# First pair prepared head by head, first two heads' minima and marks re-ordered, scores eight slots behind their minima

## The chip, the cores and the metric

One NeuronCore of a Trainium2 chip runs the whole program. The metric is device time in microseconds (us) of one execution; the kernel before has a median of 839.23 us over three executions (838.45 to 841.17).

## The reference, cut to what matters

Clustered attention (2 batches, 8 heads, 768 tokens, head width 64, 16 centroids a head), then two feed-forward blocks:

```python
q_assign = argmax(q_n @ c_n.T); k_assign = argmax(k_n @ c_n.T)     # q_n, k_n, c_n: rows over their norm
mask     = q_assign[..., :, None] == k_assign[..., None, :]
scores   = where(mask, q @ k.T / 8, -1e9)
attn     = softmax(scores);  x = attn @ v                          # heads side by side: 1536 x 512
x = ((x @ w1) * (x @ w2)) @ w3 @ w_out                             # 512 -> 1024 -> 1024 -> 512
y = softplus(x @ w_in) @ w_out2                                    # 512 -> 2048 -> 512
```

## The kernel before, in words

Heads go two by two: 16 heads are 8 pairs, pair `pi` holds heads `2*pi` and `2*pi+1`. A head has six *slots* of work, one for each 128 queries, 96 slots in all. The attention's main loop is one Python loop over a step `s`, in a manual schedule: each engine's instructions stand in the order in which the loop writes them. A step does, in this order, the **minima** of slot `s` (`mx_pe`: two matmuls of queries against keys, `mx_red`: VectorE takes the minimum of 128x768, since scores are kept negated), the row of minima of a head (`m_row`, every sixth step: transpose, negate, a DMA of 3 KB into row 96 of the head's query tile), the preparation of coming pairs (tables `PE` and `EV`, and `PE1`, `EV1` for pair 1), the **scores** of slot `s - ML` (`st_pe`: four matmuls, the second of each pair with row 96 in it; `st_exp`: ScalarE), and the **values** of the slot before that one (`av_pe`). `ML` is 9. From step 9 on, `w_step` puts in a piece of the product `w3 @ w_out`, which is computed here as 24 units (`wseq`: 8 of `w_out`, 16 of `w3`), one every 5/2 steps.

Preparing a pair takes: loads of q and k (`load_qk`, tile `rawqk`); transposes (`t1_pe`, unit `u` is half a head: u = 0, 1 the first head, 2, 3 the second) that ScalarE and VectorE copy out as a rounded part `H` and a remainder `L` (`t1_ev`); DMAs that lay `H` and `L` into the query and key tiles `q` and `k` (`t_dma`, seven DMAs a head, 1.18 MB by the shapes in the code); the squares of q and k (`norm_sq`), their sums, roots and reciprocals (`norm_sum`, `norm_root`, `norm_rec`); products with the centroids (`sims_pe`, tile `cst`), copied to `sT` (`sims_ev`) and turned (`simsT_pe`); `assign`, a chain of VectorE operations that ends in one-hot marks `oh`; `back_pe`, which turns the marks; and their copy into rows 96 on of `q` and `k`, for pair 0's first head straight from PSUM (`back_ev`), for the others by way of `sg` and DMAs (`m_dma`). A head's minima cannot start before its marks have landed. Ahead of the loop stand the centroids' preparation (`centroid_prep`, `centroid_turn`), pair 0's preparation for both heads at once, and four weight units.

All loads and copies go through SyncE's (SP's) queue in program order, unless `act_dma` names ScalarE's. PSUM tiles are `sb` (scores, and every second minimum of the first nine slots), `mb` (minima), `avb` (values), and three banks `rb` that `take` and `give` hand round.

Of the kernel before, what the change touches and what calls it, by code (L numbers as in the profile page):

```python
# [27 lines left out]
def fused_kernel(ctx: ExitStack, tc, q, k, v, centroids, w1, w2, w3, wo, w_in, w_o2, out):  # L28
# [132 lines left out]
    woh = xp_.tile([P, CC, DM], F32R, tag="x1", name="woh")  # L161

    def xs_of(c, bl):

        o, e = bl * BLK, bl * BLK + BLK
        for b in range(B):
            lo, hi = max(o, b * S), min(e, b * S + S)
            if lo < hi:
                yield slice(lo - o, hi - o), XT[b][:, c, lo - b * S : hi - b * S]
# [64 lines left out]
    def centroid_turn():  # L234
# [45 lines left out]
    def norm_root(pi):  # L280

        fl = PR["n", pi].rearrange("p t c n j -> p t (c n j)")
        nc.vector.tensor_scalar_max(fl[:, 1], fl[:, 0], 1e-30)
        nc.scalar.activation(fl[:, 2], fl[:, 1], AF.Ln)
        nc.scalar.activation(fl[:, 1], fl[:, 2], AF.Exp, scale=0.5)

    def norm_rec(pi, i):
        fl = PR["n", pi].rearrange("p t c n j -> p t (c n j)")
        if i == 0:
            nc.vector.reciprocal(fl[:, 2], fl[:, 1])  # L290
        elif i == 1:
            nc.gpsimd.tensor_tensor(out=fl[:, 0], in0=fl[:, 0], in1=fl[:, 2], op=ALU.mult)
            nc.gpsimd.tensor_tensor(out=fl[:, 0], in0=fl[:, 0], in1=fl[:, 1], op=ALU.add)
        else:
            nc.vector.tensor_scalar(
                out=fl[:, 2], in0=fl[:, 0], scalar1=0.5, scalar2=1e-6,
                op0=ALU.mult, op1=ALU.add,
            )
            nc.vector.reciprocal(fl[:, 3], fl[:, 2])

    def t1_pe(pi, u):
# [5 lines left out]
        m = take()  # L307
# [7 lines left out]
    def t1_ev(pi, u):  # L315
# [3 lines left out]
        hv, lv = PR["H", j][:, sl], PR["L", j][:, sl]  # L319
        nc.scalar.activation(hv, m[:, :HALF], AF.Copy, scale=qkcol[:, 0:1])  # L320
        nc.vector.scalar_tensor_tensor(
            out=lv, in0=m[:, :HALF], scalar=qkcol[:, 0:1], in1=f32(hv),
            op0=ALU.mult, op1=ALU.subtract,
        )
        give(m)

    def t_dma(pi, j):
# [5 lines left out]
        if hd:  # L333
# [3 lines left out]
        if hd:  # L337
            dma(f32(qt[:D]), a[:D].unsqueeze(1).to_broadcast([D, 2, S]))
            dma(f32(kt[:D, 0, :]), a[D:])
        else:  # L340
            dma(f32(qt[:D, 1, :]), a[:D])
        dma(f32(kt[:D, 1, :]), l[D:])
        for n in range(2 if hd else 1):
            n = 1 - n
# [8 lines left out]
    def t_first():  # L353

        a, l = f32(PR["H", 0]), f32(PR["L", 0])
        t_tiles(0)
        act_copy(QT[0][:D, 0, :], a[:D])
        act_copy(KT[0][:D, 0, :], a[D:])
        nc.gpsimd.tensor_copy(KT[0][D : D + 32, 0, :], a[D : D + 32])
        nc.gpsimd.tensor_copy(QT[0][D : D + 32, 0, :], l[:32])  # L360

    SG = ((0, 512), (512, S))

    def sims_pe(pi, g):
# [6 lines left out]
        for j in range(2):  # L371
            for t in (PR["H", j], PR["L", j]):
                nc.tensor.matmul(
                    m[:, : c1 - c0], cst[:, h0 + j, :], t[:, c0:c1],
                    start=(n == 0), stop=(n == 3),
# [9 lines left out]
    NG = 4  # L385
    NA = NG * QC

    NS = NA * NCL

    def simsT_pe(pi):  # L390
        PR["sx"] = take()
        for c in range(QC):
            nc.tensor.matmul(
                PR["sx"][:, c * NG * NCL : (c + 1) * NG * NCL],
                PR["sT"][:, c * P : (c + 1) * P], halves.rearrange("p g b -> p (g b)"),
# [3 lines left out]
    def assign(pi, i):  # L399

        s = PR["sx"][:, :NS].rearrange("p (a b) -> p a b", b=NCL)
        tt = nc.vector.tensor_tensor
        if i == 0:
            mx = PR["mx"] = ap1.tile([P, 2, NA], F32, tag="mx", name=f"mx{pi}")
            rn = PR["n", pi].rearrange("p t c n j -> p t (c n j)")[:, 3]
            tt(out=s, in0=s, in1=rn.unsqueeze(2).to_broadcast([P, NA, NCL]), op=ALU.mult)
            nc.vector.tensor_reduce(out=mx[:, 0], in_=s, op=ALU.max, axis=AX.X)
            tt(
                out=s, in0=s, in1=mx[:, 0].unsqueeze(2).to_broadcast([P, NA, NCL]),
# [22 lines left out]

    def back_ev(pi):

        if pi == 0:
            for ni, d in enumerate((QT, KT)):
                r = slice(64 * ni, 64 * ni + 32)
                nc.scalar.activation(
                    d[0][96:, 0, :], PR["bk"][r, :S], AF.Copy, scale=bigcol[r, 0:1]
                )  # L440
# [138 lines left out]
    NWSTEP = 5 * (NW - 1) // 2 + 11  # L579
# [30 lines left out]
    ML = 9  # L610
# [4 lines left out]
    def mx_bank(s):  # L615

        return sbank if s < ML and s % 2 else mbank

# [88 lines left out]
    def x_norm(u):  # L707
        g, hf = divmod(u, 2)
        b, h = divmod(g, H)
        if b not in XT:  # L710
            assert wk[0] > NWSTEP - 4
            XT[b] = xp_.tile([P, CC, S], F32, tag="x1", name="xT1")
# [3 lines left out]
            out=XT[b][rs, h // 2, cs],  # L716
# [155 lines left out]
    def steps(tab, s):  # L872
        for pi in range(2, NPAIR):
            for d in (0, 2):
                for f, *a in tab.get(s - 2 * QC * pi - d, ()):
                    if (d == 2) == (pi == 2 and f in NORM) and (f is not load_qk or pi > 2):
# [7 lines left out]
    EV1 = {  # L884
        0: [(t1_ev, 0), (norm_sq, 0)], 1: [(t1_ev, 1), (norm_sum, 0)], 2: [(t1_ev, 2), (norm_sq, 1), (t_dma, 0)],
        3: [(t1_ev, 3), (norm_sum, 1), (norm_root,)], 4: [(sims_ev, 0), (norm_rec, 0), (norm_rec, 1)],
        5: [(sims_ev, 1), (norm_rec, 2), (t_dma, 1)], 7: [(assign, 0)], 8: [(assign, 1)],
        9: [(back_ev,)], 10: [(m_dma, 0), (m_dma, 1)],
# [3 lines left out]
    WALL = "AbdsThlmpqe"  # L892
    WSLOT = 76
    W0 = 4
    wk = [W0]

    with tc.manual_schedule():
# [14 lines left out]
        t1_ev(0, 2)  # L912
        t1_ev(0, 3)
        centroid_turn()
        norm_sq(0, 0)
        norm_sq(0, 1)
        load_qk(1)
        t_first()
        sims_pe(0, 0)
        sims_pe(0, 1)  # L920
        sims_ev(0, 0)
        sims_ev(0, 1)
        norm_sum(0, 0)
        norm_sum(0, 1)
        simsT_pe(0)
        norm_root(0)
        for n in range(W0):
            w_step(n, WALL[:1])
        norm_rec(0, 0)
        norm_rec(0, 1)  # L930
        norm_rec(0, 2)
        t_dma(0, 1)
        t_dma(0, 0)
        assign(0, 0)
        assign(0, 1)
# [3 lines left out]
        w_load()
        load_v(0)  # L940
        for n in range(W0):
            w_step(n, WALL[1:])
        for s in range(NSLOT + ML + AL):
            j = s - ML
            a = j - AL
            if s < NSLOT:
                mx_pe(s)
                mx_red(s)
            if s and s % QC == 0 and s <= NSLOT:
                m_row(s // QC - 1)  # L950
            weights = s >= ML
# [4 lines left out]
            for tab in (PE1, EV1):  # L956
                for f, *x in tab.get(s, ()):
                    f(1, *x)
            if s == 4:
                load_qk(2)  # L960
            if s == 8:
                load_v(1)
            steps(PE, s)
            steps(EV, s)
            if 0 <= j < NSLOT:
                st_pe(j)
                st_exp(j)
            if weights:
# [7 lines left out]
            for g in range(NH):  # L976
                r = s - (ML + AL + QC * g + QC - 1)
# [7 lines left out]

            if wk[0] > NWSTEP and s >= WSLOT:
                i, k = divmod(s - WSLOT, 3)
# [8 lines left out]
    for g in range(NH):  # L996
        r0 = NSLOT + ML + AL - (ML + AL + QC * g + QC - 1)
# [199 lines left out]
```

## Time and profile before

| | us |
|---|---|
| median of three executions | 839.23 (838.45 to 841.17) |
| profiled execution, its own time | 842.76 |
| its span in the trace | 840.9 |
| first minima start on PE | 27.85 |
| first minima of head 1, of head 2 | 38.51, 58.03 |
| attention's last matmuls give way to the feed-forward block | 368 to 370 |

PE is TensorE's matmuls, DVE VectorE, ACT ScalarE, POOL GpSimd, SP SyncE. A row of the timeline gives start and duration; "[1.97 <-ACT k L438]" behind it is the engine's idle time just before and what ended it. The chain of waits is followed back from the last instruction, so an entry there is on the path that ended last.

### The profile page before, as it was taken

Reading aid. Unit: us, or ns where it says so; the run is one execution under the profiler, and the core shown is the slowest. Engines: PE = TensorE matmul, PEld = TensorE weight load, DVE = VectorE, ACT = ScalarE, POOL = GpSimd, SP = SyncE. Lnnn points to the kernel's source line nnn. Section 1 sums busy time; section 2 is a strip of 40 time slices with the busy share of each in tenths; the row PEclk is TensorE's granted clock in tenths of the full one; section 3 lists DMA queues with packets and bytes.
Section 4 is the critical chain, followed back from the end, with each engine's and each line's share of the span. In section 5 each row is a group of like instructions: output and inputs, shape, how many; then the busy total and the mean of one; then the engine's idle time right before and its main releaser. Section 6 shows DMA issues by size and latency. Waiting matters only on the chain.

```text
span 840.9 us, 10003 instructions
## 1 busy us (share of the span) xinstructions
PE 796.8 (95%) x3553; PEld 635.5 (76%) x3553; DVE 450.6 (54%) x754; ACT 396.5 (47%) x683; POOL 240.7 (29%) x232
## 2 busy tenths in 40 slices
PE   3679999989999999999999999999998999999997
PEld 2457777867777777778888888887786888888886
DVE  5867565475756565335332343345878644454443
ACT  3345445455453445455333245345555544454443
POOL 4145241245223122145201213222444222222220
PEclk9679999999999999999999999999999999999999
DMA  6875665465552564026301224330210100001001
GB/s 162 203 154 154 161 147 161 122 148 157 152 121 67 133 156 120 21 90 204 127 1 50 83 69 130 120 101 1 75 51 1 50 1 1 1 12 39 1 0 51
DMA packets 77490, 75.60 MB, mean 90 GB/s; under 512 B 46336, under 2 KB 62848, under 8 KB 77440
## 3 DMA queue, kind: packets, MB, share of 16 engines
q1 hardware_dynamic: 75476, 73.84, 32.5%
q10 hardware_dynamic: 1964, 1.12, 0.5%
q8 instruction: 28, 0.46, 0.2%
q14 instruction: 22, 0.18, 0.1%
HBM read 50.41 MB, written 3.24 MB: 64 GB/s over the span
## 4 chain that ended last, share of the span: by engine, by line
PE 77%; DVE 13%; DMA 3%; ACT 3%; SPq 2%; issue 2%; POOL 1%; DVEq 0%; ACTq 0%; POOLq 0%
PE avb L668 11%; PE rb L834 8%; PE sb L834 8%; PE sb L653 6%; PE sb L1059 6%; PE mb L1128 6%; PE rb L1059 5%; PE rb L533 5%; PE mb L856 4%; PE mb L623 3%; PE rb L1128 3%; PE avb L1128 3%; DVE mn L632 2%; PE avb L856 2%; PE rb L856 2%
## 5 line engine op out<-in xcount | busy, mean ns | idle before, releaser
L668 PE MATMUL avb<-E,v 128*128 128x384 f32 x384 | 142.7, 494 | 0.4 <-ACT t L61 0.4
L632 DVE TENSOR_REDUCE mn<-mb 128x1 f32<-128x768 f32 x92 | 87.7, 953 | 103.4 <-PE mb L623 103.0
L76 POOL TENSOR_TENSOR u<-u,t 128x512 f32<-128x512 f32 x47 | 66.2, 1409 | 173.1 <-DVE u L1082 173.1
L660 ACT ACTIVATE E<-sb 128x768 f32<-128x768 f32 x96 | 77.6, 808 | 70.1 <-PE sb L653 69.2
L653 PE MATMUL sb<-q,k 128*128 128x384 f32 (+1 forms) x384 | 91.4, 361 | 4.5 <-ACT E L660 4.5
L668 PEld LDWEIGHTS avb<-E,v 128*128 128x128 f32 x384 | 71.9, 192 | 28.7 <-ACT t L61 2.3
L653 PEld LDWEIGHTS sb<-q,k 128*128 128x128 f32 (+1 forms) x384 | 67.3, 194 | 9.6 <-ACT E L660 7.2
L623 PE MATMUL mb<-k,q 128*128 128x384 f32 x184 | 65.9, 440 | 8.0 <-DVE mn L632 4.1
L1059 PE MATMUL sb<-ys,wh_i 128*128 128x512 f32 x192 | 64.1, 395 | 3.6 <-ACT t L1070 2.9
L1072 DVE TENSOR_SCALAR u<-t 128x512 f32<-128x512 f32 x48 | 25.5, 531 | 71.3 <-ACT t L1071 71.3
L1059 PE MATMUL rb<-ys,wh_i 128*128 128x512 f32 x192 | 63.4, 392 | 0.0
L834 PE MATMUL rb<-xs,wh 128*128 128x512 f32 x192 | 61.7, 393 | 0.0
L834 PE MATMUL sb<-xs,wh 128*128 128x512 f32 x192 | 61.7, 392 | 0.0
L76 POOL TENSOR_TENSOR wl_o<-d_o,wh_o 128x512 fp32r<-128x512 f32 x16 | 21.2, 1327 | 122.3 <-ACT wh_o L61 116.2
L623 PEld LDWEIGHTS mb<-k,q 128*128 128x128 f32 x184 | 34.1, 198 | 26.7 <-DVE mn L632 7.2
L1081 ACT ACTIVATE u<-u 128x512 f32<-128x512 f32 x48 | 30.4, 633 | 42.4 <-DVE t L1078 42.2
L715 POOL TENSOR_TENSOR xT<-t,R 64x384 f32<-64x384 f32 x32 | 33.3, 1061 | 52.6 <-DMA R<-rd 52.3
L79 DVE TENSOR_TENSOR gl<-u,gh 128x512 fp32r<-128x512 f32 x48 | 37.8, 788 | 15.7 <-ACT gh L61 15.2
L1059 PEld LDWEIGHTS sb<-ys,wh_i 128*128 128x128 f32 x192 | 35.9, 188 | 13.3 <-ACT t L1070 3.9
L1059 PEld LDWEIGHTS rb<-ys,wh_i 128*128 128x128 f32 x192 | 36.1, 188 | 8.0
L834 PEld LDWEIGHTS rb<-xs,wh 128*128 128x128 f32 x192 | 36.1, 188 | 7.8
L834 PEld LDWEIGHTS sb<-xs,wh 128*128 128x128 f32 x192 | 36.1, 188 | 7.8
(202 smaller groups left out, 1730.9 us busy)
## 6 DMA issues: line engine op xcount, KB each, us to landing
w3r<-in_moe_w_dram SPq DMA_DIRECT2D x16, 512.0 KB
w12r<-in_moe_w_dram SPq DMA_DIRECT2D x16, 512.0 KB
wir<-in_moe_w_in_dram SPq DMA_DIRECT2D x16, 512.0 KB
wor<-in_moe_w_out_dram SPq DMA_DIRECT2D x16, 512.0 KB
q<-H SPq DMA_DIRECT2D x15, 384.0 KB
w3r<-in_moe_w_out_dram SPq DMA_DIRECT2D x8, 512.0 KB
k<-L SPq DMA_DIRECT2D x16, 192.0 KB
v<-in_v_dram SPq DMA_DIRECT2D x16, 192.0 KB
```

Source lines behind the costliest of these rows:

```text
L76: nc.gpsimd.tensor_tensor(out=o, in0=i, in1=hi, op=ALU.subtract)
L79: return nc.vector.tensor_tensor(out=o, in0=i, in1=hi, op=ALU.subtract)
L533: nc.tensor.matmul(m, a[:, ks], bb, start=(mc == 0 and x == 0), stop=(mc == NK - 1 and x == 2))
L623: nc.tensor.matmul(bank[:, hf, :HALF], QT[g][:, 0, c * P : (c + 1) * P], KT[g][:, 0, hf * HALF : (hf + 1) * HALF], start=True, stop=True,)
L632: nc.vector.tensor_reduce(out=MN[g][:, c : c + 1], in_=mx_bank(s)[:, :, :HALF], op=ALU.min, axis=AX.XY)
L653: nc.tensor.matmul(sbank[:, i, :HALF], KT[g][: P - 31 * n, n, ks], QT[g][: P - 31 * n, n, qs], start=(n == 0), stop=(n == 1),)
L660: nc.scalar.activation(E[j], sbank[:, :, :HALF], AF.Exp, scale=-1.0)
L668: nc.tensor.matmul(avbank[:, :HALF], V[g][:, 2 * kp + i, :], e[:, i, :], start=(kp == 0 and i == 0), stop=(kp == 2 and i == 1),)
L834: nc.tensor.matmul(bk[:, :BLK], a[:, sl], bb, start=(n == 0), stop=(n == 3 * CC - 1))
L856: nc.tensor.matmul(ybank[e][:, :BLK], a[:, es], bb, start=(fc == 0 and n == 0), stop=(fc == NFC - 1 and n == 2),)
L1059: nc.tensor.matmul(hbank[(bl * NF2 + fc) % 4][:, :BLK], a[:, sl], bb, start=(n == 0), stop=(n == 3 * CC - 1))
L1128: nc.tensor.matmul(ob, a[:, sl], bb, start=(fc == 0 and n == 0), stop=(fc == NF2 - 1 and n == 2),)
```

## The change

Pair 0 is now prepared one head at a time: the second half of norms, products, `assign` and `back_pe` for head 1 moves into the loop (table `PE0`, `EV0`). The loop's step is now called `o`. Steps 0 to 11 do minima 0 to 11, steps 12 and 13 none, steps 14 to 16 two each, and from step 17 on the minimum is `o + 1`, while scores are `o - 7` and values `o - 8`. Pair 1's preparation moves from steps 0 to 10 to steps 6 to 13, pair 2's has tables of its own (steps 12 to 21). Weight units start at step 14 with one every 9/4 steps and none are worked on before the loop. Head 0's query and key tile is filled by DMA instead of by ACT and POOL; the rounded part of `cst` is written by ACT; the centroids are loaded on ACT's queue; the attention results of batch 1's first two heads get a tile of their own (`xT10`).

```diff
     def centroid_load():
-        dma_in(PR["cw"], centroids.rearrange("h c d -> (h c) d"))
+        nc.scalar.dma_start(PR["cw"], centroids.rearrange("h c d -> (h c) d"))
...
-                nc.vector.tensor_scalar(
-                    out=hi, in0=mv[:, :, j, :], scalar1=sc, scalar2=None, op0=ALU.mult
-                )
+                act_copy(hi, mv[:, :, j, :], scale=sc)
...
+    def back_first():
+
+        r = slice(0, 32)
+        nc.scalar.activation(QT[0][96:, 0, :], PR["bk"][r, :S], AF.Copy, scale=bigcol[r, 0:1])
+        nc.vector.tensor_copy(KT[0][96:, 0, :], PR["bk"][64:96, :S])
+        give(PR["bm"])
...
-            for x in WT[wseq[n][0]].get(k - 5 * n // 2, ""):
+            for x in WT[wseq[n][0]].get(k - 9 * n // 4, ""):
...
-    ML = 9
+    ML = 8
...
-        0: [(t1_pe, 0)], 1: [(t1_pe, 1)], 2: [(t1_pe, 2)], 3: [(t1_pe, 3)], 4: [(sims_pe, 0)],
-        5: [(sims_pe, 1)], 6: [(simsT_pe,)], 9: [(back_pe,)],
+        6: [(t1_pe, 0)], 7: [(t1_pe, 1)], 8: [(t1_pe, 2)], 9: [(t1_pe, 3)], 10: [(sims_pe, 0)],
+        11: [(sims_pe, 1)], 12: [(simsT_pe,)], 13: [(back_pe,)],
...
+        12: [(assign, 0), (assign, 1)], 13: [(back_ev,), (m_dma, 0), (m_dma, 1)],
...
+    PE2 = {
+        13: [(t1_pe, 0)], 14: [(t1_pe, 1)], 15: [(t1_pe, 2)], 16: [(t1_pe, 3)],
+        17: [(sims_pe, 0), (sims_pe, 1)], 18: [(simsT_pe,)], 21: [(back_pe,)],
+    }
...
-    WSLOT = 76
-    W0 = 4
+    WSLOT = 81
+    W1 = 14
...
-        w_load()
-        w_load()
         t1_pe(0, 0)
         t1_pe(0, 1)
         centroid_prep()
+        norm_sq(0, 0)
+        norm_sq(0, 1)
         t1_ev(0, 0)
         t1_ev(0, 1)
+        centroid_turn()
         t1_pe(0, 2)
-        t1_pe(0, 3)
...
+        t1_pe(0, 3, avbank)
+        t1_hi(0, 2)
+        t1_hi(0, 3)
+        t_dma(0, 0, [0])
         load_qk(1)
...
+        norm_sum(0, 0)
+        sims_pe(0, 0, [0])
+        sims_pe(0, 1, [0])
+        norm_root(0, 0)
+        t1_lo(0, 2)
...
+        simsT_pe(0, slice(0, 4, 2))
+        for _ in range(3):
+            w_load()
+        load_v(0)
+        assign(0, 0, 0)
+        assign(0, 1, 0)
+        back_pe(0)
+        t1_lo(0, 3)
+        t_dma(0, 1)
+        back_first()
...
+        PE0 = {
+            0: [(sims_pe, 0, [1]), (sims_pe, 1, [1])], 1: [(simsT_pe, J1)], 4: [(back_pe,)],
+        }
+        EV0 = {
+            0: [(sims_ev, 0), (sims_ev, 1), (norm_rec, 0, 1), (norm_rec, 1, 1)],
+            1: [(norm_rec, 2, 1)], 2: [(assign, 0, 1)], 3: [(assign, 1, 1)],
+            4: [(back_ev,), (m_dma, 1)],
+        }
+        firsts = [[i] for i in range(12)] + [[], [], [12, 13], [14, 15], [16, 17]]
+        for o in range(NSLOT + ML + AL - 1):
+            s = o + 1 if o >= len(firsts) else -100
+            mxs = firsts[o] if s < 0 else [s] if s < NSLOT else []
+            j = o - ML + 1
...
+            if s < 0:
+                if o in (6, 12):
+                    m_row(o // 6 - 1)
+            elif s % QC == 0 and s <= NSLOT:
...
             if 0 <= j < NSLOT:
                 st_pe(j)
                 st_exp(j)
+            for i in mxs[1:]:
+                mx_pe(i)
+                mx_red(i)
```

The program order itself, at three places. First PE, from head 0's turned marks on. In these rows `mb` and `sb` with k and q are minima, `rb<-identF,rawqk` are transposes, `rb<-H,cst` and `rb<-L,cst` products with the centroids, `rb<-halves,sT` their turn. Before:

```order
L430 MATMUL rb_102<-identB,oh 128x128
L623 MATMUL mb<-k_213,q_212 128x384 x2
L309 MATMUL rb_100<-identF,rawqk_207 128x128 x3
L623 MATMUL sb<-k_213,q_212 128x384 x2
L309 MATMUL rb_101<-identF,rawqk_207 128x128 x3
```

The same place of the changed program:

```order
L440 MATMUL rb_101<-identB,oh 128x128
L634 MATMUL mb<-k_203,q_202 128x384 x2
L379 MATMUL rb_102<-H_1_192,cst 128x512
L379 MATMUL rb_102<-L_1_193,cst 128x512
L379 MATMUL rb_100<-H_1_192,cst 128x256
L379 MATMUL rb_100<-L_1_193,cst 128x256
L634 MATMUL sb<-k_203,q_202 128x384 x2
L396 MATMUL rb_101<-halves,sT_288 128x32 x6
```

Between head 0's minima stood the transposes of pair 1; now the second half of pair 0's own preparation stands there, and head 1's minima wait for its end.

Second PE, up to the first minimum of head 2 (`k_333` before, `k_391` now). `sb<-q,k` are scores, `avb<-E,v` values, `rb<-identB,oh` turned marks. Before:

```order
L623 MATMUL mb<-k_250,q_249 128x384 x2
L309 MATMUL rb_100<-identF,rawqk_366 128x128 x3
L653 MATMUL sb<-q_212,k_213 128x384 x4
L668 MATMUL avb<-E_486,v_0_285 128x384 x2
L623 MATMUL mb<-k_333,q_332 128x384 x2
```

The changed program:

```order
L440 MATMUL rb_100<-identB,oh 128x128
L318 MATMUL rb_101<-identF,rawqk_420 128x128 x3
L664 MATMUL sb<-q_268,k_269 128x384 x4
L679 MATMUL avb<-E_511,v_0_247 128x384 x2
L634 MATMUL mb<-k_391,q_390 128x384 x2
```

Ahead of that minimum stand now the scores of slots 0 to 6 (the last one is head 1's, tiles `q_268` and `k_269`) and the values of slots 0 to 5; before it was scores 0 to 2 and values 0 and 1. The turned marks of pair 1 are now just ahead of it.

Third SP's queue, up to the marks of heads 2 and 3 (`q<-sg`, `k<-sg`; `mr` is a head's row of minima). Before:

```order
L346 DMA k_382<-H_1_323 32x768
L588 DMA v_0_423<-in_v_dram 128x6x64
L588 DMA v_1_426<-in_v_dram 128x6x64
L91 DMA w3r_466<-in_moe_w_dram 128x1024
L448 DMA q_332<-sg_449 32x768
L448 DMA k_333<-sg_449 32x768
```

The changed program:

```order
L361 DMA k_446<-H_1_383 32x768
L692 DMA sd_468<-t_466 1x384
L654 DMA q_268<-mr_486 1x6x128
L459 DMA q_390<-sg_521 32x768
L459 DMA k_391<-sg_521 32x768
```

The loads of values and weights are gone from the place ahead of the marks; a head's sums (`sd`) and head 1's row of minima have come in.

## Rows read from the trace of the kernel before

**Rows 1.** Busy time by stretch: length, engines (instructions), granted clock, DMA share, GB/s.

```profile
0.00:60.00 60.00, 33.15 (x142) 26.13 (x143) 40.85 (x100) 23.36 (x43) 20.49 (x33) 0.82 0.77 176
100.00:370.00 270.00, 262.54 (x1217) 202.19 (x1215) 150.68 (x253) 132.53 (x223) 75.96 (x87) 0.99 0.48 120
```

**Rows 2.** The chain of waits up to head 2's first minimum: start, duration, what.

```profile
1.48 4.62 DMA rawqk<-in_k_dram
...
15.21 2.91 PE rb L373 x8
...
27.85 0.98 PE mb L623 x2
...
51.49 6.41 DMA k<-sg
...
58.03 0.58 PE mb L623 x2
```

**Rows 3.** The timeline around heads 1 and 2.

```profile
38.51 0.54 PE L623 MATMUL mb<-k,q 128*128 128x384 f32 x2
...
39.98 1.34 ACTq L643 DMA_DIRECT2D q<-mr  x1
...
47.49 0.90 ACT L442 ACTIVATE sg<-rb,bigcol 128x768 fp32r<-128x768 bf16 x1 [2.97 <-PE rb L430]
```

**Rows 4.** Groups by line from 0 to 62 us: count, busy, mean ns.

```profile
L632 DVE TENSOR_REDUCE mn<-mb 128x1 f32<-128x768 f32 x9 | 8.5, 945 | 6.1 <-PE mb L623 6.1
...
L320 ACT ACTIVATE H<-rb,qkcol 128x384 fp32r<-128x384 f32 x12 | 6.9, 579 | 11.2 <-PE rb L309 8.4 <-PE sb L623 1.5 <-DMA k<-H 1.2
...
L260 ACT ACTIVATE sq<-rawqk 128x768 f32<-128x768 f32 x2 | 1.7, 835 | 0.0
```

**Rows 5.** The timeline of the start: start, duration, engine, operation.

```profile
7.82 2.89 POOL L258 TENSOR_TENSOR sq<-rawqk 128x768 f32<-128x768 f32 x2
...
9.72 1.83 DVE L230 TENSOR_SCALAR cn<-cw,cs 128x64 f32<-128x64 f32 x2
...
15.24 0.23 DVE L249 SCALAR_TENSOR_TENSOR cst<-rb,cst 64x64 fp32r<-64x64 f32 x1
...
15.49 1.82 DVE L276 TENSOR_REDUCE nrm<-sq 128x12 f32<-128x768 f32 x2
...
21.32 0.57 DVE L406 TENSOR_TENSOR rb<-rb,nrm 128x384 f32<-128x384 f32 x1
...
25.07 0.80 PE L430 MATMUL rb<-identB,oh 128*128 128x128 bf16 x6 [5.54 <-DVE oh L420]
...
25.91 0.89 ACT L438 ACTIVATE q<-rb,bigcol 32x768 fp32r<-32x768 bf16 x1 [5.79 <-PE rb L430]
```

**Rows 6.** The last head's row of minima, and what waited for its DMA, on ACT's timeline.

```profile
350.16 0.27 ACT L63 ACTIVATE mr<-rb 6x128 fp32r<-6x128 f32 x1 [0.53 <-PE rb L639]
...
352.21 0.49 ACT L61 ACTIVATE t<-avb 128x384 f32<-128x384 f32 x1 [0.47 <-DMA q<-mr]
```

**Rows 7.** DMA by stretch: granted clock, DMA share, GB/s.

```profile
6.00:8.00 2.00, 1.00 1.02 369
14.00:26.00 12.00, 0.81 0.95 208
```

**Rows 8.** PE's timeline in slots with scores and values alone.

```profile
354.87 1.45 PE L668 MATMUL avb<-E,v 128*128 128x384 f32 x4
...
356.86 1.45 PE L668 MATMUL avb<-E,v 128*128 128x384 f32 x4
```

**Rows 9.** PE's clock after the wait for head 2: busy, granted clock, DMA.

```profile
60.00:62.00 2.00, 2.00 (x5) 0.50 0.22 52
```

**Rows 10.** The page's first line.

```profile
span 840.9 us, 10003 instructions
```

**Rows 11.** Head 2's row of minima, from ACT to SP's issue.

```profile
77.99 0.27 ACT L63 ACTIVATE mr<-rb 6x128 fp32r<-6x128 f32 x1 [0.95 <-PE rb L639]
...
81.06 0.79 SPq L643 DMA_DIRECT2D q<-mr  x1
```

More of the change, by code (lines that the diff above doesn't have):

```diff
@@ L161, in fused_kernel, with xt @@
     woh = xp_.tile([P, CC, DM], F32R, tag="x1", name="woh")
+    XT[1, 0] = xp_.tile([P, S], F32, tag="x10", name="xT10")
+    def xt(b, c):
+        return XT[0][:, c] if b == 0 else XT[1, 0] if c == 0 else XT[1][:, c - 1]
     def xs_of(c, bl):
@@ L278, in norm_sum, with norm_root, norm_rows, norm_rec @@
         )
[L280 to L288, printed above, removed]
+    def norm_root(pi, j=None):
+        fl = norm_rows(pi, j)
+        nc.vector.tensor_scalar_max(fl[1], fl[0], 1e-30)
+        nc.scalar.activation(fl[2], fl[1], AF.Ln)
+        nc.scalar.activation(fl[1], fl[2], AF.Exp, scale=0.5)
+    def norm_rows(pi, j):
+        n = PR["n", pi]
+        if j is None:
+            return [n[:, t].rearrange("p c n j -> p (c n j)") for t in range(4)]
+        return [n[:, t, :, :, j].rearrange("p c n -> p (c n)") for t in range(4)]
+    def norm_rec(pi, i, j=None):
+        fl = norm_rows(pi, j)
         if i == 0:
-            nc.vector.reciprocal(fl[:, 2], fl[:, 1])
+            nc.vector.reciprocal(fl[2], fl[1])
         elif i == 1:
-            nc.gpsimd.tensor_tensor(out=fl[:, 0], in0=fl[:, 0], in1=fl[:, 2], op=ALU.mult)
-            nc.gpsimd.tensor_tensor(out=fl[:, 0], in0=fl[:, 0], in1=fl[:, 1], op=ALU.add)
+            e = nc.gpsimd if j is None else nc.vector
+            e.tensor_tensor(out=fl[0], in0=fl[0], in1=fl[2], op=ALU.mult)
+            e.tensor_tensor(out=fl[0], in0=fl[0], in1=fl[1], op=ALU.add)
         else:
             nc.vector.tensor_scalar(
-                out=fl[:, 2], in0=fl[:, 0], scalar1=0.5, scalar2=1e-6,
-                op0=ALU.mult, op1=ALU.add,
-            )
-            nc.vector.reciprocal(fl[:, 3], fl[:, 2])
-    def t1_pe(pi, u):
+                out=fl[2], in0=fl[0], scalar1=0.5, scalar2=1e-6, op0=ALU.mult, op1=ALU.add
+            )
+            nc.vector.reciprocal(fl[3], fl[2])
+    def t1_pe(pi, u, bank=None):
         j, hf = divmod(u, 2)
@@ L306, in t1_pe @@
                 PR[x, j] = ap1.tile([P, S], F32R, tag=f"{x}{j}", name=f"{x}{pi}_{j}")
-        m = take()
+        m = take() if bank is None else bank
         for i in range(3):
@@ L313, in t1_pe, with t1_hi, t1_lo @@
         PR["t1", u] = m
-    def t1_ev(pi, u):
+    def t1_hi(pi, u):
+        j, hf = divmod(u, 2)
+        nc.scalar.activation(
+            PR["H", j][:, HALF * hf : HALF * hf + HALF], PR["t1", u][:, :HALF],
+            AF.Copy, scale=qkcol[:, 0:1],
+        )
+    def t1_lo(pi, u):
         j, hf = divmod(u, 2)
@@ L318, in t1_ev, with t_dma @@
         sl = slice(HALF * hf, HALF * hf + HALF)
-        hv, lv = PR["H", j][:, sl], PR["L", j][:, sl]
-        nc.scalar.activation(hv, m[:, :HALF], AF.Copy, scale=qkcol[:, 0:1])
         nc.vector.scalar_tensor_tensor(
-            out=lv, in0=m[:, :HALF], scalar=qkcol[:, 0:1], in1=f32(hv),
+            out=PR["L", j][:, sl], in0=m[:, :HALF], scalar=qkcol[:, 0:1], in1=f32(PR["H", j][:, sl]),
             op0=ALU.mult, op1=ALU.subtract,
         )
-        give(m)
-    def t_dma(pi, j):
+        if m is not avbank:
+            give(m)
+    def t1_ev(pi, u):
+        t1_hi(pi, u)
+        t1_lo(pi, u)
+    def t_dma(pi, j, ns=range(2)):
         hd = 2 * pi + j
         a, l = f32(PR["H", j]), f32(PR["L", j])
-        if hd:
+        if ns[0] == 0:
             t_tiles(hd)
@@ L336, in t_dma @@
         dma = nc.sync.dma_start
[L337 to L344, printed above, removed]
+        for n in ns:
+            if n == 0:
+                dma(f32(qt[:D]), a[:D].unsqueeze(1).to_broadcast([D, 2, S]))
+            dma(f32(kt[:D, n, :]), l[D:] if n else a[D:])
             dma(f32(qt[D : D + 32, n, :]), l[32 * n : 32 * n + 32])
@@ L370, in sims_pe @@
         n = 0
-        for j in range(2):
+        for j in js:
             for t in (PR["H", j], PR["L", j]):
@@ L374, in sims_pe @@
                     m[:, : c1 - c0], cst[:, h0 + j, :], t[:, c0:c1],
-                    start=(n == 0), stop=(n == 3),
+                    start=(n == 0), stop=(n == 2 * len(js) - 1),
                 )
@@ L615, in mx_bank @@
     def mx_bank(s):
-        return sbank if s < ML and s % 2 else mbank
+        return sbank if s < QC and s % 2 else mbank
     def mx_pe(s):
@@ L709, in x_norm @@
         b, h = divmod(g, H)
-        if b not in XT:
-            assert wk[0] > NWSTEP - 4
-            XT[b] = xp_.tile([P, CC, S], F32, tag="x1", name="xT1")
+        if b and h == 2 and hf == 0:
+            assert wk[0] >= NWSTEP
+            XT[1] = xp_.tile([P, CC - 1, S], F32, tag="x1", name="xT1")
         rs = slice(D * (h % 2), D * (h % 2) + D)
@@ L715, in x_norm @@
         nc.gpsimd.tensor_tensor(
-            out=XT[b][rs, h // 2, cs],
+            out=xt(b, h // 2)[rs, cs],
             in0=TT.pop(u)[rs], in1=R[g // 2][rs, cs], op=ALU.mult,
@@ L939, in fused_kernel @@
[L939 to L944, printed above, removed]
-            a = j - AL
[L946 to L949, printed above, removed]
+        t_dma(0, 0, [1])
+        norm_rec(0, 0, 0)
+        norm_rec(0, 1, 0)
+        norm_rec(0, 2, 0)
+        simsT_pe(0, slice(0, 4, 2))
+        for _ in range(3):
+            w_load()
@@ L950, in fused_kernel @@
                 m_row(s // QC - 1)
-            weights = s >= ML
+            weights = o >= W1
             if weights:
@@ L955, in fused_kernel @@
                 av_ev(a // 3 - 1)
[L956 to L959, printed above, removed]
+            for pi, tabs in enumerate(((PE0, EV0), (PE1, EV1), (PE2, EV2))):
+                for tab in tabs:
+                    for f, *x in tab.get(o, ()):
+                        f(pi, *x)
+            if o == 7:
+                load_v(1)
+            if o == 9:
                 load_qk(2)
-            if s == 8:
-                load_v(1)
+            if o == 16:
+                load_qk(3)
             steps(PE, s)
@@ L984, in fused_kernel @@
                 feed.load(3)
-            if wk[0] > NWSTEP and s >= WSLOT:
-                i, k = divmod(s - WSLOT, 3)
+            if o >= WSLOT:
+                assert wk[0] > NWSTEP
+                i, k = divmod(o - WSLOT, 3)
                 if i < 2:
```

120 lines of the change are left out of this document (50 added, 70 removed).

## The prediction, on record before the changed kernel ran

> **What bounds the kernel now.** I read the table of stretches first. From 100 to 370 us PE, the matrix engine, is busy 262.5 of 270 us at a granted clock of 0.99, and in the first 60 us only 33.2 of 60 at 0.82 [rows 1]. So the attention's long middle is as long as its matmuls, and what can be won or lost lies in the start. The chain of waits says what the start waits for. Head 0's queries and keys land at 6.1 us; products with the centroids start at 15.21; the first minima stand at 27.85; and head 2's first minimum waits 6.41 us for the DMA of its marks and starts at 58.03 [rows 2]. Head 1's stands at 38.51 [rows 3]. The reader is to see a string of small steps on DVE, ACT and PE, hardly ever two at once, with two transfers of marks in it.
>
> Since PE is the bound once work is there, I compare the two kernels at one place, head 2's first minimum. What counts is when PE gets there and how much other work it has done by then.
>
> **Step A, up to the first minima: 19.0 us instead of 27.85.** Head 0's data land as now. Transposes end at 7.8, the two copies of H at 0.58 each [rows 4] at 8.4 for the second transposed half, and the two of L, which I take as long as H's, at 9.0. The centroids' `cn` is no later: its two operations took 1.83 while POOL squared q and k, two squares in 2.89 [rows 5]; the squares now start at the landing, and held behind the whole first one `cn` ends at 7.7. The `cst` part now alternates between ACT and DVE, four rounds; the DVE half of a round is 0.23 [rows 5], and with as much on ACT and two hand-overs I take 0.55, so 2.2 in all, begun at 8.7 and done at 10.9. DVE's sum of squares takes 0.91 for one head (1.82 for two [rows 5]) to 11.8. Then come root, reciprocal and their small parts, about nine operations of 0.2 to 0.3, with the copies to `sT` and the turn beside them: 2.3, to 14.1. `assign` went from 21.32 to 25.07, 3.75 us for two heads [rows 5]; one head's half I put at 2.1, above one half because each of its seven operations has a fixed part. That is 16.2. Turning the marks is not halved: 0.8 [rows 5], to 17.0. The two copies of marks stay one after the other, at 0.89 [rows 5]: 18.9.
>
> The program as built makes DVE's copy wait for ACT's, because both read one PSUM bank, and no row of before shows two engines on one bank. The Trainium skill ("PSUM — Partial Sum Buffer", section "PSUM bank collisions raise a hardware error") says that two engines may be in one bank at once if they are in different quadrants of its partitions; these two are (0 to 31 and 64 to 95). By that page they could overlap and the minima start at 18.1. The wait is in the program, so the sum keeps 19.0.
>
> What leaves this stretch: ACT's and POOL's four copies that filled head 0's tile, and the weight pieces ahead of the loop. They cost nothing where they go: DMAs fill the tile while DVE is in its norms, and the weights come back from step 14 on, where PE sets the pace.
>
> **Step B, to head 1's first minimum: 33.6 instead of 38.51.** What was done beforehand for head 1 now lies between. At the half clock that PE has after such a pause (two minima took 0.98 at 27.85 [rows 2]) PE does the first minima by 20.0, head 1's products by 22.4 (half of the eight that took 2.91 [rows 2], slower), the second minima by 23.4 and the turn by 24.2. On DVE two more minima at 0.945 [rows 4] and `assign` in two halves, 2.3 with the half clock's gap of 0.7, end at 29.2. Turn 0.8, copy to `sg` 0.90 [rows 3], two issues and a landing. For that landing the trace has two ends: 6.41 in a full queue [rows 2], and for a row of minima on an empty queue 350.16 to 352.21, 2.05 with ACT's own part in it [rows 6]. The queue is nearly empty here, so I take 2.6: 33.6.
>
> The transfers allow it, narrowly. By the shapes in the code the tile of head 0 (1.18 MB), pair 1's load (0.79), values (0.39) and head 1's tile (1.18) go at 208 GB/s [rows 7], 17.0 us; three weight loads (1.57 MB) go at 369 [rows 7], 4.3 us. From 9.9 on they end at 31.2. Weights and values stand ahead of head 1's tile on SP, and pair 1's load ahead of head 0's second half; all are in this sum. With full-queue landing, or with rates a tenth lower, head 1 starts at 36 to 37.
>
> **Step C, to head 2's first minimum: 61.4 instead of 58.03.** Eight steps. PE's work in them at full clock: six scores with values at 1.99, the pitch of a slot without minima (354.87 to 356.86 [rows 8]), 11.9; a seventh scores, 0.65; six minima, 0.54 alone [rows 3] and about 0.35 in the pipeline, 2.1; five sets of transposes, 2.0; pair 1's products and turn, 2.9; marks and two rows of minima, 1.0. Sum 20.5. What is added to it:
> - At its start ACT is in the way: minimum 1.0, transposed row 0.3, its copy 0.3, the row's DMA issued on ACT 1.34 [rows 3], two H at 0.58, two squares at 0.84 [rows 4]. The first exponential ends at 40.2; PE has had 3.0 of its 20.5 by then. The rest, 17.5, ends at 57.7.
> - `assign` of pair 1, 3.75, is now in one step. Scores and values (1.99) cover a part: 1.8 more.
> - The marks' copy 0.9 and landing 2.4 stand against transposes, scores and values, 2.4: 0.9 more.
> - One stretch at half clock after PE's pause at 36 to 40, 1.0 (in 60 to 62 PE ran 2.00 of 2 us at 0.50 [rows 9]). The like after head 2's wait falls on both kernels.
>
> That is 61.4. Bounds: 58 if the clock holds and `assign` is hidden, 65.5 if the marks land as slowly as now.
>
> Ahead of this place PE has then done scores 3 to 6 and values 2 to 5 more than before, four times 1.99, and three sets of transposes fewer (1.2): 6.8 us of work. So 58.0 - 61.4 + 6.8 = 3.4 in hand.
>
> **Step D, the rest.** The same work is left on each engine, in 90 steps instead of 94, and PE bounds it: 7.5 us idle in 270 [rows 1]. The 24 weight units take 62 steps instead of 64 and end five steps later counted from the start, still well ahead of the end; they add nothing. `xT10` is a place in memory. I carry 3.4 through: the profiled execution (842.76 in all, span 840.9 [rows 10]) would go to 839.4, and against the median of 839.23 that is **835.8 us**.
>
> **Rivals.** A difference under 0.3%, 2.5 us, can hardly be told from none here.
> - *Marks of head 2 eat it.* If they land in 6.4 instead of 2.4, or SP reaches them late behind head 3's tile, 4.0 goes: 839.8, no change. For it: that is what the chain shows today. Against it: of what stood on SP between head 3's tile and the marks, two value loads and a 512 KB weight load are gone, and two transfers of a few KB have come.
> - *Scores run into their own row of minima.* With eight slots instead of nine a head's row has two steps, 3.98 [rows 8], less 0.4 for what stands ahead in the first of them; ACT to landing is 2.05 [rows 6]. That leaves 1.5. But for head 2 SP issued the row only at 81.06, 2.8 after ACT had it at 78.26 [rows 11]. It decides where SP is later than 1.5: at 2.8 each such head costs 1.3, and at the 4.0 that a blocked queue can hold it, 2.5. Three heads cost 4 to 7, six cost 8 to 15: 840 to 848, slower. Against it: the sums that SP waits for ahead of the row are written one step sooner, relative to the row, than before.
> - *The pauses are covered.* Half clock never comes and DVE's chains fit: 58.0 at head 2, 7 in hand, 832; with step B two earlier, 830.
> - *The minima start early and nothing follows.* Step C swallows steps A and B whole, as head 2's marks are held by transfers: this ends within 1 us of the first rival.
>
> **Chances.** My forecast with the third rival 0.54 (the third alone 0.14), the first and fourth 0.28, the second 0.18. Hence faster by over 0.3% 0.53, within 0.29, slower 0.18. The range is 830.5 (all pauses covered) to 841.5: it takes in the first rival and the mild end of the second and leaves out its far end and a little of the third.
>
> **What to look for.** First minima at 17.5 to 20.5; head 1's at 32 to 37; head 2's at 58 to 65.5 with six values ahead of it; the feed-forward block's first matmuls at 364 to 366 instead of 368 to 370. A wait of scores for a DMA of `mr`, at head after head, would show the second rival, and a long DMA of `sg` ending a wait at 60 the first. I am wrong in the base if PE's idle time from 100 us on is more than 3 us off 7.5: then the middle is not PE's alone.

## The result, and the profile after

The change made the kernel slower: 849.02 us median over seven executions (847.13 to 850.78) against 841.17 for the kernel before beside it (838.45 to 844.94), a ratio of 1.0088 with a 95% interval of 1.0061 to 1.0114. The forecast was 835.8. The feed-forward block's first matmul starts at 374.19 us; in the trace of before it starts at 368.22, and 364 to 366 was forecast. So 6.0 of the 6.2 us between the profiled spans (847.1 and 840.9) were lost ahead of that block.

The stretches of [rows 1] in the changed kernel:

```profile
0.00:60.00 60.00, 38.74 (x168) 30.31 (x168) 34.59 (x97) 19.45 (x40) 13.77 (x24) 1.00 0.69 162
100.00:370.00 270.00, 259.30 (x1200) 197.60 (x1198) 153.35 (x259) 130.90 (x220) 76.93 (x86) 0.99 0.49 126
```

PE is 5.6 us busier in the first 60 us: it has more to do there, as meant, and part of its work took longer. The granted clock of 1.00 in the first row can't be taken at its word before some 40 us: in the turn at 13.10 each matmul record starts 0.214 us after the one before, which is the pace of rows with a granted clock of 0.50; at 1.00 it is 0.112 (see the experiment on the halved turn). From 100 us on PE is idle for 10.7 us where it was 7.5, so the middle is no longer as long as its matmuls.

The chain of waits of the start, to be held against [rows 2]: start, duration, what.

```profile
13.10 2.79 PE rb L396 x12
18.46 0.81 PE rb L440 x6
19.29 0.90 ACT q L446
20.21 0.97 DVE k L447
21.22 1.01 PE mb L634 x2
...
36.34 0.98 PE mb L634 x2
...
61.56 2.13 DMA k<-sg
63.83 0.59 PE mb L634 x2
```

First minima at 21.22 (27.85 before), head 1's at 36.34 (38.51), head 2's at 63.83 (58.03), each some 2.5 us later than forecast.

**An account by slots.** To find where the middle went I took the trace matmul by matmul. A slot j runs from the first scores of step j to those of step j+1. I priced its matmuls by the median pitch from start to start of their kind between 100 and 360 us (0.176 us for a matmul record of scores or minima, 0.322 for one of values, 0.231 for one of 512 columns, 0.109 for a transposed square of f32). Matmuls are pipelined and a record is longer than its pitch (0.34 for the scores' 0.18), so a wait of up to 0.16 us hides in busy time. What a slot takes above its price is lost. These prices and losses are my own sums from the trace, not lines of a view. The table has the start of slot 0, the price of slots 0 to 94, and what was lost in groups of slots, in us; the last four columns are experiments told below.

| | before | after | t first | w3ol first | both | before, lead 8 |
|---|---|---|---|---|---|---|
| slot 0 starts at | 47.7 | 39.7 | 38.4 | 39.5 | 39.6 | 46.4 |
| price of the work | 296.9 | 302.0 | 302.0 | 302.0 | 302.0 | 297.9 |
| lost in slots 0-16 | 7.5 | 9.8 | 12.0 | 9.8 | 10.1 | 5.6 |
| 17-35 | 2.4 | 3.5 | 2.1 | 3.5 | 2.2 | 4.6 |
| 36-39 | 6.3 | 0.8 | 0.7 | 0.8 | 0.8 | 7.9 |
| 40-48 | 0.9 | 3.1 | 3.0 | 3.7 | 2.8 | 2.2 |
| 49-66 | 2.3 | 10.9 | 7.6 | 6.9 | 3.3 | 5.2 |
| 67-94 | 2.1 | 2.4 | 2.0 | 2.5 | 1.7 | 7.6 |
| lost in all | 21.6 | 30.6 | 27.6 | 27.2 | 20.8 | 33.0 |

Scores start 8.1 us earlier with 5.1 us more work left for the loop: 3.0 in hand at that place. (The forecast's 3.4 is meant at another place, head 2's first minimum; the section on the prediction comes back to it.) Then the loop loses 9.0 more than before, and 8.6 of that in slots 49 to 66. Before had a stall of its own, in slots 36 to 39, which is not there after the change: ACT's copy `H` waited for transfers that still read the old one, as this row of before shows.

```profile
189.50 0.58 ACT L320 ACTIVATE H<-rb,qkcol 128x384 fp32r<-128x384 f32 x1 [4.03 <-DMA k<-H]
```

PE's waits in that region of the changed kernel, from 200 to 300 us: who waited for what, us in all, times, longest.

```profile
PE rb L318 <- DVE w3ol L79: 1.6, 1, 1.6
PE rb L379 <- DVE w3ol L79: 1.6, 1, 1.6
PE avb L679 <- ACT t L61: 1.5, 2, 1.0
PE rb L650 <- DVE oh L425: 1.2, 1, 1.2
PE mb L634 <- DVE mn L643: 1.1, 3, 0.5
PE sb L664 <- ACT E L671: 0.8, 1, 0.8
```

In the same stretch of before the profile has one line alone, for the transpose of `mn`:

```profile
PE rb L639 <- DVE oh L420: 1.8, 2, 1.2
```

The others are new. The two largest of them, the waits for `w3ol` and for `t`, can both be seen in one slot, 52. PE's timeline (start, duration; in brackets the idle time before and what ended it):

```profile
231.37 1.45 PE L679 MATMUL avb<-E,v 128*128 128x384 f32 x4
...
233.01 0.27 PE L650 MATMUL rb<-identF,mn 128*6 128x128 f32 x1
233.03 0.97 PE L664 MATMUL sb<-q,k 128*128 128x384 f32 x4
234.48 1.56 PE L679 MATMUL avb<-E,v 128*128 128x384 f32 x4 [0.48 <-ACT t L61]
...
239.02 0.59 PE L634 MATMUL mb<-k,q 128*128 128x384 f32 x2
241.26 0.50 PE L379 MATMUL rb<-H,cst 128*128 128x512 f32 x1 [1.65 <-DVE w3ol L79]
```

ACT's timeline, then DVE's:

```profile
233.32 0.27 ACT L63 ACTIVATE mr<-rb 6x128 fp32r<-6x128 f32 x1 [0.88 <-PE rb L650]
233.49 0.57 ACT L61 ACTIVATE w3oh<-rb 128x512 fp32r<-128x512 f32 x1
233.97 0.46 ACT L61 ACTIVATE t<-avb 128x384 f32<-128x384 f32 x1
```

```profile
239.65 0.96 DVE L643 TENSOR_REDUCE mn<-mb 128x1 f32<-128x768 f32 x1 [4.59 <-PE mb L634]
240.53 0.68 DVE L79 TENSOR_TENSOR w3ol<-rb,w3oh 128x512 fp32r<-128x512 f32 x1
```

**The first theory** reads ACT's rows. `m_row` is issued when s is a multiple of six, `av_ev` when a is a multiple of three. With nine slots of lead a is s - 10, and the two never share a step; with eight a is s - 9, and every sixth step holds both. What the copy `t` reads is there from 232.8 on (the values at 231.37 and their 1.45), but it stands on ACT behind `mr`, which waits for PE's transpose of the newest minima, and behind the step's weight copies, and PE's next values wait for `t`. The Trainium skill ("PSUM — Partial Sum Buffer", section "Engine vs sequencer instructions") says that ACT's and DVE's queues are strictly first in, first out; these rows agree, with ACT idle up to 233.32 and `t` begun only at 233.97. That the weight copies alone are not the cause can be read in before: there, too, `t` stands behind them, but never in the step of `mr`, and the profile has PE wait for it once, 0.4 us. The lost time in front of the values stands at slots 22, 28, 34 and so on to 82: 0.16 to 0.18 us with `mr` alone ahead, 0.65 with a weight copy as well, 1.13 at slot 58; 4.9 from slot 16 on.

**The second theory** reads DVE's. Three PSUM banks (`rb`) serve transposes, products and weights. At a weight unit every 9/4 steps, two units' products and a third's transposes can hold all three, and the next to want one waits for `w3ol`, the last operation of the oldest unit. DVE stands idle for 4.59 us, since `w3ol` was written behind the step's minimum, which PE reaches only after twelve products and a transposed tile.

**The third**, a rival to both: PE's half clock (0.93 granted from 250 to 275 us) after pauses that come by chance.

### The profile page after: what moved, and what is told of

It is laid out like the page before. It is cut to its first block, busy times and chain, and to the rows that moved or that the text cites. A ratio compares the mean times of both kernels' runs of the same rounds, so it can differ in the third digit from the quotient of the medians.

```text
span 847.1 us, 10047 instructions
## 1 busy us (share of the span) xinstructions
PE 802.3 (95%) x3571; PEld 635.7 (75%) x3571; DVE 449.0 (53%) x766; ACT 395.8 (47%) x688; POOL 238.7 (28%) x228
## 4 chain that ended last, share of the span: by engine, by line
PE 78%; DVE 12%; ACT 3%; DMA 2%; issue 2%; SPq 1%; POOL 1%; ACTq 0%; DVEq 0%; POOLq 0%
PE avb L679 12%; PE rb L845 8%; PE sb L845 8%; PE sb L664 6%; PE sb L1099 6%; PE mb L1168 6%; PE rb L1099 5%; PE rb L544 5%; PE mb L867 4%; PE mb L634 4%; PE rb L1168 3%; PE avb L1168 3%; PE avb L867 2%; PE rb L867 2%; PE rb L396 2%
## 5 line engine op out<-in xcount | busy, mean ns | idle before, releaser
L634 PE MATMUL mb<-k,q 128*128 128x384 f32 x186 | 68.3, 449 | 10.7 <-DMA k<-sg 6.4
L634 PEld LDWEIGHTS mb<-k,q 128*128 128x128 f32 x186 | 33.9, 198 | 33.6 <-DVE mn L643 9.4
```

The lines of the kernel that those rows point to most:

```text
L634: nc.tensor.matmul(bank[:, hf, :HALF], QT[g][:, 0, c * P : (c + 1) * P], KT[g][:, 0, hf * HALF : (hf + 1) * HALF], start=True, stop=True,)
```

## The experiments

**The copy t first.** In each step `av_ev` is moved ahead of `m_row` and the weights.

```diff
+            if a > 0 and a % 3 == 0:
+                av_ev(a // 3 - 1)
             if s < 0:
                 if o in (6, 12):
                     m_row(o // 6 - 1)
...
                 w_step(wk[0], "hlpqe")
-            if a > 0 and a % 3 == 0:
-                av_ev(a // 3 - 1)
```

> Every sixth step the copy of the values' bank (t, on ACT) stands behind the copy of the row of minima (mr), which waits for a transpose that waits for a minimum. Here t stands ahead of mr and of the weights' work in each step; nothing else is moved. Theory 1 (the eight-slot lead puts the two copies in one step, and the scores times values wait for t at slots 22, 28, 34 and so on to 82, 0.16 to 1.13 us each, 4.9 in all in the profile): about 4 us faster than the changed kernel, 844 to 846, and these waits gone. Theory 2 (the weights' 9/4 pace runs out of PSUM banks): no change, 849. Theory 3 (the half clock alone): no change but by chance.

844.99 us median (840.46 to 846.12), ratio to before 1.0024 (1.0009 to 1.0039): 4.0 us won. In the view of the values' bank, over the whole span, the changed kernel has this line for PE's waits, and here there is none:

```profile
  ACT t L61: 2.9, 5
```

(The line counts only what is left idle after a matmul's modelled end, hence less than 4.9.) The waits for `w3ol` stand as they were, 1.6 and 1.6. As the first theory has it.

**The last operation of a unit first.** `w3ol` is issued ahead of the step's minimum.

```diff
+            if o >= W1:
+                w_step(wk[0], "e")
             for i in mxs[:1]:
                 mx_pe(i)
...
-                w_step(wk[0], "hlpqe")
+                w_step(wk[0], "hlpq")
```

> At slots 52 and 61 PE waits 1.8 us each for a bank that the last operation of a weight unit (w3ol, on DVE) gives back; that operation stands on DVE behind the step's minimum, which PE delivers only after twelve products and a turn. Here w3ol stands ahead of the minimum in every step. Theory 2 (banks run out at the 9/4 pace): 3 to 4 us faster, 845 to 846, both waits gone, and the waits for t as before. Theory 1: no change beyond 1 us.

845.53 us (842.77 to 847.95), ratio 1.0038 (1.0024 to 1.0053): 3.5 won. PE's waits from 200 to 300 us have no `w3ol` left, and `t` stays. (The longest wait for `mn` has grown from 0.5 to 1.6 us.)

```profile
PE mb L634 <- DVE mn L643: 1.9, 2, 1.6
PE avb L679 <- ACT t L61: 1.4, 2, 1.0
```

**Both.**

> The changed kernel with both edits at once: the copy t ahead of the copy mr, and w3ol ahead of the minimum. If the two causes are separate places that PE pays one after the other, the two gains (4.0 and 3.5 us) add: 841 to 842.5, and the loss of PE after slot 16 falls to some 13 us from 21. If one pause hid in the other: 843 to 845.

839.49 us (837.77 to 840.31), ratio 0.9964 (0.9952 to 0.9977): 9.5 us below the changed kernel and 2.4 below before. By the ratios the first edit wins 0.64%, the second 0.50% and both 1.24%, so the two add, within their intervals; slots 49 to 66 lose 3.3 instead of 10.9. From slot 17 on 10.7 are lost, against 20.8 in the changed kernel. From 100 to 370 us, and from 200 to 300, where the changed kernel's PE was busy for 92.15 us, it reads

```profile
100.00:370.00 270.00, 264.88 (x1239) 204.22 (x1238) 156.49 (x262) 137.41 (x229) 82.03 (x91) 1.00 0.52 131
200.00:300.00 100.00, 96.89 (x470) 75.50 (x470) 64.50 (x108) 47.74 (x82) 32.42 (x38) 1.00 0.51 119
```

That is 5.1 us idle from 100 us on, and the feed-forward block begins at 364.42.

**The old pace of the weights.**

```diff
-            for x in WT[wseq[n][0]].get(k - 9 * n // 4, ""):
+            for x in WT[wseq[n][0]].get(k - 5 * n // 2, ""):
...
-    WSLOT = 81
-    W1 = 14
+    WSLOT = 84
+    W1 = 11
```

> The weights at the old pace of a unit every 5/2 steps, from step 11 on so that they end three steps later than at 9/4. Theory 2: the waits for w3ol at two slots go (3.6 us), 845 to 846. Theory 1: these waits may go, but the waits for t at every sixth slot stay, and no more than 3.6 is won; if the pace were nothing, 849.

848.14 us (844.21 to 849.99), ratio 1.0063 (1.0039 to 1.0086): 0.9 won, within the spread. The waits for `w3ol` are gone, and slots 49 to 66 lose 3.8 instead of 10.9, but slots 67 to 94 lose 6.7 instead of 2.4, and slots 0 to 16 lose more too. In the late slots DVE waits 4.55 us for a row of sums, where it waited 0.58 in the changed kernel, and the minimum behind it on DVE holds PE:

```profile
329.05 0.86 DVE L704 TENSOR_SCALAR r<-r 128x6 f32<-128x6 f32 x1 [4.55 <-DMA r<-sd]
```

```profile
331.03 1.01 PE L634 MATMUL mb<-k,q 128*128 128x384 f32 x2 [2.79 <-DVE mn L643]
```

So the pace and the start of the weights together decide the bank waits, as the second theory has it (this edit changes both, and no run parts them). The gain was given back elsewhere, behind a transfer that landed later; why it did is not shown.

**The lead of eight in the kernel before.**

```diff
-    ML = 9
+    ML = 8
```

> The kernel before with minima eight slots ahead of the scores instead of nine, and nothing else changed. Theory 1: the copy t and the copy mr fall into one step here too, and the kernel is 3 to 4.5 us slower than before: 844 to 846, with waits for t at every sixth slot. Theory 2 and theory 3: the same as before within 1 us, 840 to 842.

850.48 us (847.68 to 855.55), ratio 1.0107 (1.0077 to 1.0137): 8.7 us slower, twice what I expected. The waits for `t` came to every sixth slot (5.3 us, summed as above), with this at slot 52:

```profile
249.69 1.56 PE L668 MATMUL avb<-E,v 128*128 128x384 f32 x4 [0.98 <-ACT t L61]
```

The rest lies where engines wait for transfers: slots 36 to 39 lose 7.9 instead of 6.3, and slots 67 to 94 lose 7.6 instead of 2.1 (the row of sums again). The execution that was profiled took 854.99, 4.5 above the median, so these losses are larger than in most.

**The same with the copy t first** (the edit of the first experiment).

> The kernel before with the lead of eight slots (850.5 us), and the copy t ahead of the copy mr in each step. The waits for t at every sixth slot summed to 5.4 us in that profile. Theory 1: 845 to 846, these waits gone; what is left over the 841.8 of before are the waits at slots 38 and 77 that do not go by t. If the lead itself costs: 849 to 850.

846.21 us (843.06 to 848.59), ratio 1.0053 (1.0034 to 1.0072): 4.3 won back, and in its trace the same values start without a wait:

```profile
242.82 1.45 PE L668 MATMUL avb<-E,v 128*128 128x384 f32 x4
```

So the line wins the same 4 us in both kernels, 4.0 and 4.3, and in the kernel before one number had put the waits in. Of the other 4 us of this lead in the kernel before, 2.6 stand in one place: at slot 77 PE waits 3.60 us for DVE, which waits 4.04 for a row of sums. With the lead of nine DVE waited 3.05 at that place, and PE only 0.99. So a shorter lead also leaves PE less room when DVE is late; that this is all of the rest is not shown.

**Second and third pair one step earlier** (on top of both edits).

```diff
-                    for f, *x in tab.get(o, ()):
+                    for f, *x in tab.get(o + (pi > 0), ()):
                         f(pi, *x)
...
-            if o == 9:
+            if o == 8:
                 load_qk(2)
-            if o == 16:
+            if o == 15:
                 load_qk(3)
```

> Both edits, and the preparation of the second and third pair one step earlier (loads too). In the changed kernel PE waits 1.9 us at slot 5 and 1.2 at slot 13 for marks in oh, and 1.7 each at slots 6 and 15 for their transfer. If one step (2.7 to 4.5 us) is what these chains lack: 3 to 5 us below both edits alone, 837 to 839, with these waits gone. If transfers on the queue hold the marks whenever they are issued: within 1 us of both edits alone.

838.32 us (836.58 to 840.19), ratio 0.996 (0.9947 to 0.9974): 1.2 below both edits, within the spread of either. PE's waits from 50 to 100 us:

```profile
PE rb L440 <- DVE oh L425: 2.7, 2, 1.5
PE mb L634 <- DVE mn L643: 1.9, 2, 1.0
PE sb L664 <- ACT E L671: 1.3, 1, 1.3
```

With both edits alone:

```profile
PE mb L634 <- DMA k<-sg: 3.9, 2, 2.4
PE rb L440 <- DVE oh L425: 2.8, 2, 1.7
```

The transfer is no longer waited for, as hoped, but PE now comes earlier to marks that DVE has not written and to minima that stand behind weight work on DVE and to scores whose exponentials stand behind norms on ACT. I expected 3 to 5 us, and most of the waits merely changed their names.

**The halved turn from one stretch of memory** (on top of both edits).

```diff
+    halfj = cpool.tile([P, 2, 2, NCL], F32, name="halfj")
+    nc.vector.tensor_copy(halfj, halves.rearrange("p (n j) b -> p j n b", j=2))
...
-        h = halves[:, js]
+        h = halves if js == slice(0, 4) else halfj[:, js.start]
```

> Both edits, and the halved turn at the start reads its 32 columns from one stretch of memory instead of two groups of 16. The turn took 2.77 us at 13.10, and the whole turn with 64 columns in one stretch took 1.60 in the kernel before, both at half clock. If the two groups are the cause: 0.8 to 1.6 us here, the first minima at 19.9 to 20.2 instead of 21.2, and the end 1 us earlier at most. If it is the small width: still 2.8, and no change.

838.48 us (837.07 to 839.69), ratio 0.9966 (0.9954 to 0.9978): 1.0 below both edits by the medians and level with them by the ratios, so nothing that can be told from their spread. In the trace the turn took 1.52 instead of 2.77 and the minima start 1.4 earlier, as the first guess had it. But the second turn of the same execution, from the same stretch of memory, took 2.60:

```profile
12.92 1.52 PE L398 MATMUL rb<-halfj,sT 128*128 128x32 f32 x12 [1.25 <-DVE nrm L304]
...
19.80 1.01 PE L636 MATMUL mb<-k,q 128*128 128x384 f32 x2 [1.97 <-DVE k L449]
...
22.53 2.60 PE L398 MATMUL rb<-halfj,sT 128*128 128x32 f32 x12
```

The two stretches by themselves (length, PE's busy time and records, granted clock, DMA share, GB/s):

```profile
12.92:14.44 1.52, 1.52 (x12) 1.00 0.66 149
22.53:25.13 2.60, 2.60 (x14) 0.50 1.17 302
```

So what parts the two lengths is the clock's level, 1.00 (2.4 GHz) at the first turn and 0.50 (1.2 GHz) at the second; between them PE had stood idle from 14.44 to 17.03. The whole turn, with 64 columns, shows the same two lengths at one place of one program, in the kernel before and in its copy with a lead of eight slots, which differ only behind it:

```profile
17.94 1.60 PE L393 MATMUL rb<-halves,sT 128*128 128x64 f32 x12
```

```profile
17.94 2.82 PE L393 MATMUL rb<-halves,sT 128*128 128x64 f32 x12
```

The first of these ran at a granted clock of 1.00 from 18.07 on, and not at half clock as I had read it when I set this experiment up. And in the run with `t` first the second turn, in two groups of 16, goes over from a pitch of 0.214 to one of 0.112 us in mid-turn. Neither guess holds: the turn's length goes by the clock, neither by its groups nor by its width, and that the number came out as the first guess had it was luck.

**All four edits.**

> All four edits: the copy t first, w3ol first, the second and third pair's preparation one step earlier, and the turn at the start from one stretch of memory. The first won 4.0 and the second 3.5 us of the changed kernel's 849.0, both together ended at 839.5, the third took that to 838.3 and the fourth to 838.5. If the last two add: 837 to 837.5. If head 1's first minimum, which waits for the transfer of its marks, takes back what the turn gives: 838 to 838.5.

838.84 us (838.04 to 839.79), ratio 0.9955 (0.9937 to 0.9973): the last two do not add. The three best versions, 838.3 to 838.8, can't be told apart, and all beat both kernels. The trace says why the turn adds nothing: with the same edit, from one stretch of memory, it is back at the length that it had without it, and the first minima start at 21.42.

```profile
13.30 2.77 PE L398 MATMUL rb<-halfj,sT 128*128 128x32 f32 x12 [1.47 <-DVE nrm L304]
```

## Why the prediction was wrong

**Step A** (19.0, measured 21.22). The order and the lengths of `cst`, sums and copies held; `cst` was done at 10.68 for 10.9. What was mis-sized is the halved turn: I left it beside root, reciprocal and small parts, in a term of 2.3 in all, and it stood behind them and alone took 2.8, at the pace of half clock. `assign` waited for it:

```profile
15.90 0.37 DVE L410 TENSOR_TENSOR rb<-rb,nrm 128x192 f32<-128x192 f32 x1 [2.17 <-PE rb L396]
```

Where the same turn met a granted clock of 1.00 it took 1.52, and the minima started at 19.80; so of the 2.2 some 1.3 (2.77 less 1.52) go with the clock, and the rest with the sum. `assign` took 2.4 for 2.1. The wait of `k`'s copy for `q`'s on one bank came as the sum had it, 0.90 and 0.97 one after the other; whether the two could overlap was not run.

**Step B** (33.6, measured 36.34). 2.2 of the 2.7 came from step A. The second turn took 2.40 where the sum had 0.8, half of the 1.60 of before: at half clock, and half the columns save nothing. The matmuls ahead of it took 2.9 where it had 4.4. From the copy `sg` to the minimum it was 3.1 us for the 2.6 taken; the 6.41 of a full queue was rightly left out.

**Step C** (27.8 from head 1 to head 2, measured 27.5). Right in sum: by the slots PE waited 1.9 us for `assign` where 1.8 was taken, and 1.7 for the marks where 0.9 was. The first rival, that head 2's marks take 4 us more, did not come.

So head 2's first minimum stood at 63.83, 5.8 later than before where 3.4 was forecast (61.4 for 58.0). By the prices of the slots PE had done 7.3 us more work ahead of it (6.8 forecast). That leaves 1.5 in hand at the forecast's own place instead of 3.4, and most of the difference comes from step A. That would still have made the kernel 1.5 us faster. From there to the last slot the loop lost 24.6 us against 17.2 before.

**Step D failed.** "The same work is left on each engine [...] and PE bounds it", I wrote, "I carry 3.4 through". The work was the same, but not its order. I had weighed the shorter lead only by a row's way to the scores (the second rival, 840 to 848; its own terms, 4 to 15 us on 835.8, reach 851, so a time like the measured one was in it by its size), and that wait was there once, with 0.4 us. The lead also sets which copies share a step on ACT, and I did not look there: 4.0 us, shown by taking it away in both kernels and by putting it into the one that did not have it. And I priced the faster weights at nothing because they end "well ahead of the end". That says nothing of the banks that they hold meanwhile: 3.5 us. The change also took 5.5 us out of slots 36 to 39, which I had not seen in before, so that the loss looked smaller than the new waits.

With both causes away the kernel is 2.4 us faster than before by the medians, 3.0 by the spans, and the feed-forward block starts at 364.42, inside the 364 to 366 of the forecast. That agreement is in part luck: in that trace 1.3 us are in hand at head 2's first minimum, and 2.5 come from a loop that loses 14.7 from there on where before lost 17.2, since the 5.5 of slots 36 to 39 that I had not seen outweigh the new waits that are left. So the middle was not as long as its matmuls in either kernel, and what it loses above them did not stay the same.

The warning that I had set, PE's idle time from 100 us on more than 3 us off 7.5, came true with 10.7. The third theory fell as an account of the loop: half clock came and went with the pauses (slot 58 in the changed kernel, 16 with `t` first, neither with both edits). A granted clock of 0.93 over 25 us comes to an estimate of 1.7 us in that one trace. At the start, in step A, it does count.

## What to carry to other kernels

When a lead, a pace or a phase between two loops changes, list for every engine which instructions now share a step, and ask of each one that is ready whether it stands behind one that is not. A stretch in which PE is busy for 97% [rows 1] is bound by PE only as long as no wait is added; a scheme with three buffers in turn is as fast as the queue in which the release of the oldest stands. Price the slots matmul by matmul before believing a busy share: small waits hide in the overlap of pipelined records. And hold two lengths of PE's work against each other only at the same granted clock.

## What the runs showed of the hardware

The turn of the products is six f32 matmuls (twelve records). At a granted clock of 1.00 its records start 0.112 us apart with 64 moving columns (the kernel before) and with 32 in one stretch (the halved turn from one stretch, at 12.92). At 0.50 they start 0.214 us apart with 32 columns in one stretch (the same run, at 22.53), and at that same pace with 32 in two groups of 16 (the changed kernel, at 13.10) and with 64 (the kernel before with a lead of eight, at 17.94). So the whole turn takes 1.5 to 1.6 us at full clock and 2.6 to 2.8 at half clock, whatever its width and layout. The Trainium skill ("TensorE: Matmul & The Clock Gate", section "Step-by-step: what each phase is for") puts the streaming of a matmul at one cycle for each column. By that the halved turn would have saved time; at these sizes the trace shows nothing saved for 32 columns less.

Which level the clock has at the start differs between executions of code that is the same up to there: with the turn from one stretch the first turn took 1.52 us in one run and 2.77 in the other.
